# Second group's queries turned by TensorE products with the identity, and an earlier first rounding step of w_in: polysketch attention with an ELU feed-forward

## The chip, the cores and the metric

The kernel runs on one core of one Trainium2 chip. The metric is the device time of one execution in microseconds (us); the time before is the median of three runs. One further execution was recorded by the hardware profiler, and every view shown here comes from that one.

## The reference, cut to what matters

Sizes: batch 4, heads 4, sequence 1088, head dimension 32, sketch r = 8, d_model 128, d_ff 2048. q, k and v are float32; S1, S2, w_in and w_out come as float64.

```python
def phi(x):
    a = np.einsum('rd,bhsd->bhsr', S1, x)
    b = np.einsum('rd,bhsd->bhsr', S2, x)
    return np.einsum('bhsi,bhsj->bhsij', a, b).reshape(*x.shape[:-1], r * r)
q_p, k_p = (phi(q), phi(k))
kv = np.einsum('bhsf,bhsd->bhfd', k_p, v)
z = np.sum(k_p, axis=2)
num = np.einsum('bhsf,bhfd->bhsd', q_p, kv)
den = np.einsum('bhsf,bhf->bhs', q_p, z)[..., None] + 1e-06
attn_out = num / den
...
x = attn_out.transpose(0, 2, 1, 3).reshape(B * S, H * D)   # 4352 x 128
h = x @ w_in
g = np.where(h > 0.0, h, np.exp(np.minimum(h, 0.0)) - 1.0)
out = g @ w_out
```

## The kernel before, in words

The 4352 rows of x are handled in groups of 512 (a group is eight half tiles of 64 sequence positions with all four heads; the last group has 256). For a group the kernel works out the sketch of its queries, the denominator, the attention output x (tile `xg`, features on partitions), then in eight steps of two blocks of 128 hidden features each: `mm1` (h = w_in block times xg, tile `h`), the ELU on ScalarE (`elu_a`, tile `e`) and VectorE (`elu_d`, tile `gg`), and the second product into `o`, `pa` or `pb`. From the third group on, and for part of the second, the second product has seven block products in place of eight, with sums on POOL.

The order of the instructions is written out by hand: an engine runs its instructions in the order in which the Python code calls them, and waits for other engines by semaphores. Lines 952 to 1006 are the head, the loop at line 1107 is the steady part, in which tables (`at`, `mid`, `late`, lines 1015 to 1104) hang further work on a step's number.

The head, as far as it bears on the change:

- Loads go out on SP's queue in the order of lines 145 to 226: S, k, the first eight half tiles of q, v, the first w_in block (`load_w(0, 0)`), the other nine half tiles of q (line 215), the next w_in block, two w_out blocks, and so on. `hd_q` holds q with heads and 32 positions on partitions, `raw` the float64 words of a weight block.
- `transp` (line 281) turns q or k on VectorE, in blocks of 32x32, into `qT` or `kT` (head and feature on partitions).
- Weights are rounded from float64 to float32 in steps: `RA` (line 101, VectorE: the high word masked), `RB` (line 106, ScalarE), then on VectorE sign, mantissa, low word (lines 116, 120, 128: `RC_2` for the first two w_in blocks together) and the final product (line 136, `RE`).
- `KF`, `KO_*`, `Z*`: features of the keys of batch 0, their outer products (tile `kp`) and their sum. `KA` (line 428) has the 36 products of v with kp into tile `kv`, `KS_first` turns it (ScalarE copy `kd`, TensorE transpose, ScalarE copy `kvS`).
- First group: `q1_first` (tile `abq`), `q1z_first` (tile `zqp`), `q2_den` (line 603 `pw`, 608 and 609 `den`, 611 `an`: the division), `q2_out` (line 624, `qp`, two halves), `q4_early` (TensorE transposes `qtp`, ScalarE copies `qpT`, line 637), `q5_early` (products `xps`, ScalarE copies `xg`, line 649), `mm1_first` (tile `h`, line 257).
- Second group: `transp(qT, "q", 0, 8, NT)` turns half tiles 8 to 16 of batch 0, `q1_second` (line 537, tile `abwp`) uses half tiles 8 to 15.
- `keep_warm` gives TensorE products of ones into the tile `idle`, which nothing reads.

PSUM tiles with the tag `h` share four buffers, those with the tag `aux` two.

Of the kernel before, what the change touches and what calls it, by code (L numbers as in the profile page):

```python
# [12 lines left out]
F32 = mybir.dt.float32  # L13
# [9 lines left out]
def _ap(ap: bass.AP, free):  # L23
    return dataclasses.replace(ap, ap=[list(ap.ap[0])] + [list(x) for x in free])
# [3 lines left out]
def kernel(  # L28
# [21 lines left out]
    nc = tc.nc  # L50
    B, H, S, D = q.shape
    R = S1.shape[0]
    P = 128
# [4 lines left out]
    NT = S // 64  # L58
# [7 lines left out]
    psum = ctx.enter_context(tc.tile_pool(name="psum", bufs=2, space=bass.MemoryType.PSUM))  # L66


    hd = {}
# [3 lines left out]
    qT = [const.tile([FD, NT, 64], F32, name=f"qT{b}") for b in range(2)] * 2  # L73
# [104 lines left out]
    def round_w(f, i, *a):  # L178
        if wide:
            cp, w_in, w_out = order[i]  # L180
            c = slice(0 if w_in else 2 * P, 4 * P if w_out else 2 * P)
            f(raw_w[cp][:, c], W[:, cp, c], *a)

    def RA(i):
        round_w(round_a, i)

    def RB(i):
        round_w(round_b, i)


    def RC_2():
        if wide:
            for f in (round_s, round_m, round_d):
                f(raw_2[:, :, :2 * P], W[:, :2, :2 * P])
# [33 lines left out]
    ident = const.tile([P, P], F32, name="ident")  # L228
# [23 lines left out]
    width = [32]  # L252
# [8 lines left out]
    def keep_warm(n, cols=256, tile=P):  # L261
        ones = nc.const_aps.tensor(1.0, [P, 256], F32)
        for i in range(n):
            for c in range(0, P, tile):
                nc.tensor.matmul(idle[c:c + tile, :cols], ones[:, :tile], ones[:, :cols], skip_group_check=True,  # L265
                                 tile_position=(0, c))
# [13 lines left out]
    def transp(dst, x, b, t0, t1):  # L280
        nc.vector.transpose(dst[b][:, t0:t1, :].rearrange("p t (a c) -> p c t a", c=2), hd[x, b][:, :, t0:t1, :])


    SXh = const.tile([P, FD], F32, name="SXh")

    def make_SXh():
# [129 lines left out]
    def z_tile(b, ps, i):  # L416
        c = 32 * (i % 4)
        ab = feats[b]
        nc.tensor.matmul(ps[c:c + 32, R * R:R * R + H * R], ab[:, 0, i].rearrange("p h r -> p (h r)"),
                         ab[:, 1, i].rearrange("p h r -> p (h r)"), start=(b == 0 and i < 4), stop=(i >= KT - 4),  # L420
                         skip_group_check=True, tile_position=(0, c))

    def KA(b):
        kv = kv_ps[b] = psum.tile([P, 512], F32, name="kv", **(dict(tag="aux") if b else dict(tag="o1", bufs=1)))
        kp = [feats.pop((b, half)) for half in range(2)]
        for i in range(KT):
            for h in range(H):
                nc.tensor.matmul(kv[32 * h:32 * h + 32, :R * R], vt[b][:, (h * KT + i) * D:(h * KT + i + 1) * D],  # L428
                                 kp[i // 5][:, i % 5, h].rearrange("p i j -> p (i j)"),
                                 start=(i == 0), stop=(i == KT - 1), skip_group_check=True, tile_position=(0, 32 * h))  # L430
            if b:
                z_tile(b, kv, i)
# [42 lines left out]
            z_tile(0, ps, i)  # L475
        return ps, ZC(0, ps)

    def KS_first():
        kd = work.tile([P, 2, R * R], F32, name="kd", tag="kd", bufs=1)
        nc.scalar.copy(kd[:], _ap(kv_ps[0][:, :R * R], [[0, 2], [1, R * R]]))  # L480
        nc.tensor.transpose(kv_ps[0][:, 128:256], kd[:].rearrange("p w f -> p (w f)"), ident[:])
        nc.scalar.copy(kvS[:].rearrange("p h d -> p (h d)"), kv_ps[0][:, 128:256])

    def KV_first():
# [38 lines left out]
    def q1z_first():  # L523
        p = psum.tile([P, 512], F32, name="zqp", tag="h", bufs=4)
        for i in range(4):
            for u in range(2):
                b, t = half_tile(0, 2 * i + u)
                nc.tensor.matmul(p[64 * u:64 * u + 64, i * 32:i * 32 + 32].rearrange("p (h r) -> p h r", h=H),
                                 qT[b][:, t, :], SW[:, :, 2, :], skip_group_check=True, tile_position=(0, 64 * u))
        return p[:, :128].rearrange("p (t h r) -> p h t r", t=4, h=H)  # L530
# [65 lines left out]
    def q2_den(g, zq=None, between=None):  # L596
        m = H * (un[g] if g > 1 else qn[g])
        x = abw[g][:, :m, :]
        pw = pws[g % 2]
        if zq is None:  # L600
            nc.vector.tensor_mul(pw[:, :m, :R], x[:, :, R:2 * R], x[:, :, 2 * R:3 * R])
        else:
            nc.vector.tensor_mul(pw[:, :m, :R].rearrange("p (h t) r -> p h t r", h=H),
                                 x[:, :, R:2 * R].rearrange("p (h t) r -> p h t r", h=H), zq)
        if between:
            between()
        den = work.tile([P, 8 * H], F32, name="den", tag="den")
        nc.vector.tensor_reduce(den[:, :m], pw[:, :m], axis=AX, op=ADD)
        nc.vector.reciprocal(den[:, :m], den[:, :m])
        an = work.tile([P, 8 * H, R], F32, name="an", tag="an")  # L610
        nc.vector.tensor_mul(an[:, :m], x[:, :, R:2 * R], _ap(den[:, :m], [[1, m], [0, R]]))
        ans[g] = an

    def q2_out(g, parts=1, between=None):
        m = H * qn[g]
        x, an = abw.pop(g), ans.pop(g)
        qp[g] = work.tile([P, 4 * H, R, R], F32, name="qp", tag="qp", bufs=2)
        for i in range(parts):
            if i and between:
                between()  # L620
            h = slice(i * m // parts, (i + 1) * m // parts)
            a_ = an[:, h]
            b_ = x[:, h, :R]
            nc.vector.tensor_mul(qp[g][:, h], _ap(a_, list(a_.ap[1:]) + [[0, R]]),
                                 _ap(b_, [b_.ap[1], [0, R], b_.ap[2]]))

    def q4_early(g):

        qpT[g] = work.tile([P, H, 2, P], F32, name="qpT", tag="qpT", bufs=2)
        for hh in range(2):  # L630
            p = psum.tile([P, 512], F32, name="qtp", tag="aux")
            for h2 in range(2):
                for m in range(2):
                    o = (h2 * 2 + m) * P
                    r = (2 * hh + h2) * 4 + 2 * m
                    nc.tensor.transpose(p[:, o:o + P], qp[g][:, r:r + 2].rearrange("p t i j -> p (t i j)"), ident[:])  # L636
            nc.scalar.copy(qpT[g][:, 2 * hh:2 * hh + 2], p[:].rearrange("p (h m s) -> p h m s", h=2, m=2))

    def q5_early(g):
        xp = [psum.tile([P, 512], F32, name="xps", tag="aux") for _ in range(2)]  # L640
        for h in range(H):
            for w in range(2):
                nc.tensor.matmul(xp[w][D * h:D * h + D, :256], kvS[64 * w:64 * w + 64, h, :],
                                 qpT[g][64 * w:64 * w + 64, h].rearrange("p m s -> p (m s)"),
                                 skip_group_check=True, tile_position=(64 * w, D * h))
        xg[g] = work.tile([P, 512], F32, name="xg", tag="xg", bufs=3)
        to = xg[g][:].rearrange("p (m w s) -> p w m s", w=2, s=P)
        for w in range(2):
            nc.scalar.copy(to[:, w], xp[w][:, :256].rearrange("p (m s) -> p m s", s=P))  # L649
# [313 lines left out]
    KO_first(7, KT)  # L963
    keep_warm(1, 96, 64)
    zq = q1z_first()
    q2_den(0, zq, lambda: RA(0))
    q2_out(0, 2, lambda: RA(1))
    KA(0)
    KS_first()
    keep_warm(1)  # L970
    RB(0)
    RB(1)
    q4_early(0)
    transp(qT, "q", 0, 8, NT)
    RC_2()
    RE(0)
    RE(1)
    q1_second()
    q5_early(0)
    keep_warm(1, 192, width[0])  # L980
    mm1_first()
    q2(1, 2, lambda: RA(2))
    RB(2)
# [39 lines left out]
    def late(n, f, *a):  # L1023
        extra.setdefault((n, 1), []).append((f, *a))
# [28 lines left out]
    for b, (n_t, n_f, n_o, n_a, n_z) in enumerate(  # L1053
            ((4, 6, (7, 9), 11, 12), (15, 16, (17, 18), 19, 20), (19, 21, (23, 24), 27, 28)), 1):
        at(n_t, transp, kT, "k", b, 0, NT)
        at(n_f, KF_late, b)
        late(n_f, KF_late_out, b)
        for half in range(2):
            if b == 1:
                at(n_o[half], KO, b, half, nc.gpsimd)  # L1060
            else:
                late(n_o[half] - 1, KO_a, b, half)
                at(n_o[half], KO_b, b, half)
        at(n_a, KA, b)
        late(n_a, sums_out, b)
        at(n_z, turn, b)
        late(n_z, turned, b)
    late(10, transp, qT, "q", 1, 0, NT)
    at(21, transp, qT, "q", 2, 0, NT)
    late(24, transp, qT, "q", 3, 0, NT)  # L1070
# [36 lines left out]
    for n in range(2, N):  # L1107
        g, cp = steps[n]
# [29 lines left out]
        g, cp = before  # L1138
# [10 lines left out]
    g = NQ - 2  # L1149
# [53 lines left out]
```

## Time and profile before

| what | value |
|---|---|
| median of three runs | 265.38 us (265.32 to 265.83) |
| the profiled execution's own time | 265.08 us |
| its span, first to last instruction | 263.3 us |
| TensorE (PE) busy | 257.8 us, 98% |
| VectorE (DVE) busy | 188.2 us, 71% |
| ScalarE (ACT) busy | 184.5 us, 70% |
| GpSimd (POOL) busy | 168.2 us, 64% |
| mean granted TensorE clock | 1.000 |

The span is counted from the first instruction; all moments are us from there. In the busy tenths a row has 40 digits, one for each 6.6 us of the span, each the busy share of that slice in tenths. The chain of waits is the work that ended last, followed back from the last instruction: start, length, engine, tile and line. In the timeline a row has start, length, engine, line, operation, the tile written and those read, the shape and the count of instructions merged into it, and in brackets the idle time before it and what ended that. PE is a matmul, PEld the load of its stationary operand, SPq and ACTq are issues of DMAs. An f32 product counts as two instructions on PE.

### The profile page before, as it was taken

The numbers are of one execution on the slowest core, as the hardware profiler recorded it, in microseconds if no ns is written. First come the engines' busy times: TensorE is split into PE (matmuls) and PEld (weight loads), VectorE is DVE, ScalarE is ACT, GpSimd is POOL, SyncE is SP. The second block draws the span as 40 slices with busy tenths as digits, with TensorE's granted clock in tenths as the row PEclk, the third lists the DMA queues.
The fourth block names the chain that finished last, engine by engine and source line by source line (L and its number), as shares of the span: only waits on it lengthen the run. The fifth ranks groups of instructions, "written<-read, shape, count | busy, mean of one in ns | idle before, by whom it ended". The sixth has DMA issues, their size and how long they took to land.

```text
span 263.3 us, 9739 instructions
## 1 busy us (share of the span) xinstructions
PE 257.8 (98%) x4127; PEld 160.5 (61%) x4127; DVE 188.2 (71%) x349; ACT 184.5 (70%) x356; POOL 168.2 (64%) x251
## 2 busy tenths in 40 slices
PE   8899999999999999999999999999999999999994
PEld 7652334354346756667666666665666666667994
DVE  6899999997969997996477676644446445674651
ACT  2479978677567656775587777776777777777793
POOL 4400009105477996798869799888688888998300
PEclk9999999999999999999999999999999999999999
DMA  5997099020011110000100110011001100110011
GB/s 176 339 349 209 2 277 230 1 72 18 2 24 26 26 20 2 2 4 17 31 3 0 29 18 0 2 19 25 3 2 21 23 4 0 18 20 8 2 30 32
DMA packets 26442, 13.73 MB, mean 52 GB/s; under 512 B 19328, under 2 KB 24576, under 8 KB 26400
## 3 DMA queue, kind: packets, MB, share of 16 engines
q1 hardware_dynamic: 25968, 12.76, 18.9%
q8 instruction: 32, 0.52, 0.9%
q10 hardware_dynamic: 368, 0.30, 0.3%
q0 software_dynamic: 64, 0.07, 0.1%
q14 instruction: 10, 0.08, 0.1%
HBM read 10.88 MB, written 2.23 MB: 50 GB/s over the span
## 4 chain that ended last, share of the span: by engine, by line
PE 96%; POOL 1%; DVE 1%; ACT 1%; issue 0%
PE h L257 44%; PE pb L792 16%; PE pa L792 13%; PE o L257 5%; PE pb L768 4%; PE ol L257 3%; PE idle L265 1%; PE kv L428 1%; PE h L686 1%; PE qps L686 1%; POOL kp L324 1%; PE kfps L360 1%; PE qps L576 1%; PE qtp L636 1%; PE kv L257 1%; PE abp L341 1%
## 5 line engine op out<-in xcount | busy, mean ns | idle before, releaser
L257 PE MATMUL h<-xg,W 128*32 128x512 f32 (+3 forms) x904 | 130.7, 539 | 0.4 <-ACT xg L649 0.4
L875 DVE SCALAR_TENSOR_TENSOR gg<-e,h 128x512 f32<-128x512 f32 x128 | 85.6, 683 | 54.1 <-ACT e L869 50.6
L867 ACT ACTIVATE e<-h 128x512 f32<-128x512 f32 x128 | 75.5, 590 | 45.6 <-PE h L257 42.9
L869 ACT ACTIVATE e<-e 128x512 f32<-128x512 f32 x128 | 80.9, 632 | 3.8
L257 PEld LDWEIGHTS h<-xg,W 128*32 128x32 f32 (+1 forms) x904 | 42.6, 122 | 43.2 <-issue 34.9
L754 POOL TENSOR_TENSOR tt<-gg 128x256 f32<-128x256 f32 x50 | 37.0, 741 | 16.4 <-DVE gg L875 16.1
L751 POOL TENSOR_TENSOR tt<-gg 128x256 f32<-128x256 f32 x50 | 36.7, 734 | 5.5 <-DVE gg L875 5.1
L755 POOL TENSOR_TENSOR tt<-tt,gg 128x256 f32<-128x256 f32 x50 | 37.5, 750 | 3.9
L756 POOL TENSOR_TENSOR tt<-gg,tt 128x256 f32<-128x256 f32 x50 | 37.2, 744 | 3.9
L792 PEld LDWEIGHTS pa<-gg,W 128*64 128x64 f32 (+1 forms) x496 | 23.8, 125 | 23.5 <-issue 22.9
L792 PE MATMUL pa<-gg,W 128*64 128x128 f32 (+1 forms) x496 | 30.5, 274 | 0.0
L792 PE MATMUL pb<-tt,SS 128*64 128x128 f32 (+1 forms) x480 | 29.5, 273 | 0.0
L792 PEld LDWEIGHTS pb<-tt,SS 128*64 128x64 f32 (+1 forms) x480 | 22.6, 126 | 0.0
L792 PE MATMUL pa<-tt,SS 128*32 128x128 f32 (+1 forms) x288 | 21.0, 273 | 0.0
L133 POOL TENSOR_TENSOR raw<-raw,tiny 128x512 f32<-128x512 f32 x1 | 1.0, 1044 | 29.4 <-DVE raw L128 29.4
L792 PE MATMUL pb<-tt,W 128*64 128x128 f32 (+1 forms) x256 | 19.8, 273 | 0.0
L792 PE MATMUL pb<-gg,SS 128*64 128x128 f32 (+1 forms) x256 | 19.8, 273 | 0.0
L257 PE MATMUL o<-gg,W 128*32 128x512 f32 x128 | 15.3, 594 | 0.0
L792 PEld LDWEIGHTS pa<-tt,SS 128*32 128x32 f32 (+1 forms) x288 | 13.6, 124 | 0.0
L792 PEld LDWEIGHTS pb<-gg,SS 128*64 128x64 f32 (+1 forms) x256 | 12.7, 125 | 0.0
L792 PEld LDWEIGHTS pb<-tt,W 128*64 128x64 f32 (+1 forms) x256 | 12.6, 125 | 0.0
L768 PE MATMUL pb<-gg,W 128*32 128x256 f32 x192 | 11.5, 380 | 0.0
(163 smaller groups left out, 279.5 us busy)
## 6 DMA issues: line engine op xcount, KB each, us to landing
raw<-in_moe_w_in_dram SPq DMA_DIRECT2D x8, 256.0 KB, 6.6
raw<-in_moe_w_out_dram SPq DMA_DIRECT2D x8, 256.0 KB, 6.4
hd_k<-in_k_dram SPq DMA_DIRECT2D x3, 544.0 KB, 7.3
hd_q<-in_q_dram SPq DMA_DIRECT2D x3, 544.0 KB, 7.9
out_dram<-ob SPq DMA_DIRECT2D x88, 16.0 KB, 1.5
v<-in_v_dram SPq DMA_DIRECT2D x4, 288.0 KB, 6.8
v<-in_v_dram SPq DMA_DIRECT2D x4, 256.0 KB, 8.3
hd_k<-in_k_dram SPq DMA_DIRECT2D x1, 288.0 KB, 3.3
```

Source lines behind the costliest of these rows:

```text
L257: nc.tensor.matmul(dst[c:c + tile], lhs[:, c:c + tile], rhs, skip_group_check=True, tile_position=(0, c), **kw)
L265: nc.tensor.matmul(idle[c:c + tile, :cols], ones[:, :tile], ones[:, :cols], skip_group_check=True, tile_position=(0, c))
L686: nc.tensor.matmul(ps[w][s * r:s * r + s, 64 * k:64 * (k + m)], lhs, qpT[g, i][rows, o + 2 * k:o + 2 * (k + m), f, :], start=(f == 0 and j ...
L751: nc.gpsimd.tensor_tensor(t[:, 0], b12, b11, op=SUB)
L754: nc.gpsimd.tensor_tensor(t[:, 2], b22, b12, op=SUB)
L755: nc.gpsimd.tensor_tensor(t[:, 1], t[:, 2], b11, op=ADD)
L756: nc.gpsimd.tensor_tensor(t[:, 3], b21, t[:, 1], op=SUB)
L768: nc.tensor.matmul(acc[1][0][r:r + width[0], 256 * hi:256 * hi + 256], lhs[:, w:w + width[0]], gg[:, c, 256 * u:256 * u + 256], start=(cp ...
L792: nc.tensor.matmul(bank[r:r + width[0], P * col:P * col + P], lhs[:, w:w + width[0]], rhs[:, u], start=(first and i in ((0,) if g == 1 els ...
L867: nc.scalar.activation(e, hs[g, cp][c][:, :n], RELU, scale=-1.0)
L869: nc.scalar.activation(e, e, EXP, scale=-1.0)
L875: nc.vector.scalar_tensor_tensor(gs[g, cp][:, c, :n], es[g, cp][:, c, :n], -1.0, hs[g, cp][c][:, :n], op0=ADD, op1=MAX)
```

## The change

Half tiles 8 to 15 of the first batch's queries are no longer turned by VectorE in the head. `turn_q` turns them on TensorE: for each half tile, each half of it and each head one 32x32 product of the q block with the identity, 32 in each of two calls, all into one PSUM tile `qtu` of 128x512; `turn_q_out` copies each half of that tile (128x256) on ScalarE into `qT`. Half tile 16, which the second group doesn't use, is turned by VectorE in step 3 of the loop. One `keep_warm` is left out and another has 128 columns in place of 192. `RA(0)` is called ahead of `q2_den`, where it stood between the division's first product and its sum. `RB(0)` is called ahead of `KA`, and the copy to `kvS` (`KS_first_b`) stands between the two ScalarE copies `qpT` of the first group.

```diff
--- before.py
+++ after.py
@@ -281,6 +281,23 @@
         nc.vector.transpose(dst[b][:, t0:t1, :].rearrange("p t (a c) -> p c t a", c=2), hd[x, b][:, :, t0:t1, :])
 
 
+
+    def turn_q(t0, t1):
+        if not turned_q:
+            turned_q.append(psum.tile([P, 512], F32, name="qtu", tag="h", bufs=4))
+        for t in range(t0, t1):
+            for c in range(2):
+                for h in range(H):
+                    r = slice(D * h, D * h + D)
+                    o = 64 * (t - 8) + 32 * c
+                    nc.tensor.matmul(turned_q[0][r, o:o + 32], hd["q", 0][r, c, t, :], ident[r, r],
+                                     skip_group_check=True, tile_position=(D * h, D * h))
+
+    def turn_q_out(t0, t1, copy=nc.scalar.copy):
+        copy(qT[0][:, t0:t1, :].rearrange("p t (a c) -> p t a c", c=2),
+             turned_q[0][:, 64 * (t0 - 8):64 * (t1 - 8)].rearrange("p (t c a) -> p t a c", c=2, a=32))
+
+    turned_q = []
     SXh = const.tile([P, FD], F32, name="SXh")
 
     def make_SXh():
@@ -475,10 +492,12 @@
             z_tile(0, ps, i)
         return ps, ZC(0, ps)
 
-    def KS_first():
+    def KS_first_a():
         kd = work.tile([P, 2, R * R], F32, name="kd", tag="kd", bufs=1)
         nc.scalar.copy(kd[:], _ap(kv_ps[0][:, :R * R], [[0, 2], [1, R * R]]))
         nc.tensor.transpose(kv_ps[0][:, 128:256], kd[:].rearrange("p w f -> p (w f)"), ident[:])
+
+    def KS_first_b():
         nc.scalar.copy(kvS[:].rearrange("p h d -> p (h d)"), kv_ps[0][:, 128:256])
 
     def KV_first():
@@ -624,7 +643,7 @@
             nc.vector.tensor_mul(qp[g][:, h], _ap(a_, list(a_.ap[1:]) + [[0, R]]),
                                  _ap(b_, [b_.ap[1], [0, R], b_.ap[2]]))
 
-    def q4_early(g):
+    def q4_early(g, between=None):
 
         qpT[g] = work.tile([P, H, 2, P], F32, name="qpT", tag="qpT", bufs=2)
         for hh in range(2):
@@ -635,6 +654,8 @@
                     r = (2 * hh + h2) * 4 + 2 * m
                     nc.tensor.transpose(p[:, o:o + P], qp[g][:, r:r + 2].rearrange("p t i j -> p (t i j)"), ident[:])
             nc.scalar.copy(qpT[g][:, 2 * hh:2 * hh + 2], p[:].rearrange("p (h m s) -> p h m s", h=2, m=2))
+            if between and hh == 0:
+                between()
 
     def q5_early(g):
         xp = [psum.tile([P, 512], F32, name="xps", tag="aux") for _ in range(2)]
@@ -963,21 +984,24 @@
     KO_first(7, KT)
     keep_warm(1, 96, 64)
     zq = q1z_first()
-    q2_den(0, zq, lambda: RA(0))
+    RA(0)
+    q2_den(0, zq)
     q2_out(0, 2, lambda: RA(1))
+    RB(0)
     KA(0)
-    KS_first()
-    keep_warm(1)
-    RB(0)
+    turn_q(8, 12)
+    KS_first_a()
+    turn_q_out(8, 12)
+    turn_q(12, 16)
+    turn_q_out(12, 16)
     RB(1)
-    q4_early(0)
-    transp(qT, "q", 0, 8, NT)
+    q4_early(0, KS_first_b)
     RC_2()
     RE(0)
     RE(1)
     q1_second()
     q5_early(0)
-    keep_warm(1, 192, width[0])
+    keep_warm(1, 128, width[0])
     mm1_first()
     q2(1, 2, lambda: RA(2))
     RB(2)
@@ -1065,6 +1089,7 @@
         late(n_a, sums_out, b)
         at(n_z, turn, b)
         late(n_z, turned, b)
+    late(3, transp, qT, "q", 0, 16, NT)
     late(10, transp, qT, "q", 1, 0, NT)
     at(21, transp, qT, "q", 2, 0, NT)
     late(24, transp, qT, "q", 3, 0, NT)
```

## The prediction

> **What bounds the kernel now.** I read four views in this order. First the page's busy tenths, which say in which stage which engine is full:
>
> ```profile
> PE   8899999999999999999999999999999999999994
> ...
> PEclk9999999999999999999999999999999999999999
> ```
>
> TensorE is full from the third slice (13 us) on, at a granted clock of 1.0. Every part of the change except one small transpose lies in the first two and a half slices, so the question is what sets the moment from which TensorE runs without a pause. The chain of waits gives that moment:
>
> ```profile
> 12.52 0.14 issue
> 12.65 0.63 PE qtp L636 x4
> 13.28 0.85 PE abwp L537 x16
> 14.13 0.70 PE xps L643 x16
> 14.83 0.64 ACT xg L649 x2
> 15.47 0.11 issue
> 15.58 2.79 PE h L257 x40
> ```
>
> From h at 15.58 us the chain stays on TensorE to the last step; read instruction by instruction, TensorE has no idle stretch above 0.03 us after 15.58 until 60 us and later. So what moves 15.58 moves the end by as much. Just ahead of it the chain is ScalarE's copy xg, ahead of that the products xps, then abwp, which reads qT of the second group. The timeline shows how close the rival input is:
>
> ```profile
> 9.43 1.21 PE L428 MATMUL kv<-kp,v 128*32 128x64 f32 x72
> 9.62 0.29 DVE L603 TENSOR_TENSOR pw<-abq,zqp 128x128 f32<-128x128 f32 x1 [0.23 <-PE zqp L528]
> 9.82 0.33 DVE L101 TENSOR_SCALAR W<-raw 128x256 uint32<-128x256 uint32 x1
> ...
> 10.07 0.29 DVE L608 TENSOR_REDUCE den<-pw 128x16 f32<-128x144 f32 x1
> ...
> 12.42 0.77 DVE L281 STREAM_TRANSPOSE qT<-hd_q 128x576 f32<-128x576 f32 x1
> ...
> 13.31 0.59 ACT L637 COPY qpT<-qtp 128x512 f32<-128x512 f32 x1 [0.28 <-PE qtp L636]
> ...
> 14.81 0.65 ACT L649 COPY xg<-xps 128x256 f32<-128x256 f32 x2 [0.15 <-PE xps L643]
> 15.01 0.76 DVE L136 SCALAR_TENSOR_TENSOR W<-raw,W 128x256 f32<-128x256 f32 x2
> ```
>
> VectorE's first weight block is done at 15.43 (half of the 0.76 us row), xg at 15.46: h waits for two engines that arrive within 0.03 us of each other. Relieving one alone brings nothing. The reader should also see that L101, the step RA(0) that the change moves, lies between pw and den and that VectorE was idle for 0.23 us before pw. Last, the landing of what RA(0) reads (its load is issued at 3.90 us):
>
> ```profile
> DMA to landing us min/median/max: 5.7/5.7/5.7
> ```
>
> It lands at 9.60, so the idle 0.23 us (9.39 to 9.62) is not free for RA(0).
>
> **What the Trainium skill says.** "TensorE: Matmul & The Clock Gate", Part 3, says that small matmuls at different tile positions overlap, with some 4 ns from tile to tile. The trace agrees for column tiles (four kv products start 7 ns apart, and the next four 55 ns later); it has no 32x32 tiles. "TensorEngine Tiling (Array Packing)", Gotcha 1, says that different row tiles cannot access one PSUM bank at the same time. The four heads of turn_q are four row groups writing one bank, though other partitions of it; no run here shows that. "VectorE: DVE Perf Modes", The DRAIN you can't avoid: the next operation starts when the pipe is empty, earlier when it isn't held. Here pw to L101 is 0.20 us, but a dependent step 0.32 (den to reciprocal). "ScalarE: Activation LUTs", What ACT_TABLE_LOAD costs: back-to-back ACTIVATEs overlap by about 93 ns; in the trace 0.10 (two xg copies of 0.37 start 0.27 apart).
>
> **The change part by part.**
>
> *RA(0) ahead of pw.* It can start at 9.60 plus the 0.07 us from landing to start (first k tile: 4.5 to 4.57), about 9.69. pw follows 0.25 later (as den follows L101 now), at 9.94, and den 0.32 after pw, at 10.26 instead of 10.07. So the move costs VectorE 0.19 us: between pw and den RA(0) lay half in a wait that had to be waited anyway. Behind the waiting RA(0) stand pw, the division and both qp halves; the second qp ends at 12.69 instead of 12.50. If the load lands 0.2 us earlier the move costs nothing, if 0.2 later 0.4.
>
> *The VectorE transpose taken out* (0.77 us at 12.42). RC_2 can follow qp at 12.69, but waits for RB(1) on ScalarE, below. VectorE is ahead of TensorE there in the end, so this gain of up to 0.5 us goes to waiting.
>
> *turn_q, twice 32 products.* An f32 product is two instructions (36 kv products stand as x72), so twice 64. In sets of four tiles that is 16 sets. The nearest row is zps, also 32 columns and 32-wide: eight instructions in two sets, the sets 0.033 us apart. kv, with 64 columns, has 0.055. I take 0.033, keep 0.055 as the upper bound, and as the lower 0.025, the floor that the TensorE page gives for a start-to-start (Wait — 56ns, not 53.3ns?). A turn is then 15 x 0.033 = 0.50 to the last start, plus 0.20 for that instruction (zps row): 0.70. The first start is 10.57: last kv start 10.42 plus the 0.15 that zqp to kv shows for another tile shape. hd_q must be there: its load is the next after RA(0)'s, 288 KB, and the loads around it land 0.7 us per 256 KB apart, so about 10.4 (estimate). That fits by 0.15 us; later landings are paid one for one, with kd's transpose and all of qtp queued behind.
>
> *The new waits.* The built program shows the second turn_q waiting for a ScalarE semaphore, and the only new ScalarE step between is the first turn_q_out: both use one bank. So the halves do not overlap. The chain, with a release of 0.07 us to ScalarE (kv end 10.64 to kd 10.71) and 0.05 to TensorE (kd end 10.98 to 11.03), and 0.37 us for a copy (abq and xg halves, also 128x256):
> - first turn 10.57 to 11.27; copy 11.34 to 11.71;
> - second turn 11.76 to 12.46; copy from 12.53;
> - on ScalarE in order, each start a duration less 0.10 later: RB(1) 12.80 (0.51), qpT 13.21 (0.59), kvS 13.70 (0.27), second qpT 13.87, done 14.46, instead of 13.90.
>
> TensorE keeps up: qtp can start at 12.4 and its second half at 12.9 (qp is there at 12.69, so RA(0)'s 0.19 is hidden), abwp runs 13.5 to 14.4. Then xps at 14.51, xg 0.75 later as now (14.06 to 14.81), h 0.77 after xg as now: 16.03. RC_2 after RB(1) starts at 13.34 instead of 13.12, weights at 15.65, ahead of xg (15.91). **h moves from 15.58 to 16.03, +0.45 us.** kvS is moved behind the first qpT and RB(0) ahead of kd; RB(0) needs 10.05 to 10.56, just before kd at 10.71, and costs nothing, the 0.17 of kvS is in the list. The removed keep_warm (0.60 us) and the narrower second one fill pauses and set no end.
>
> *The rest transpose in step 3* (128x64): the transposes shown fall by 0.9 ns per element, so 0.25 us, 0.2 after overlap. VectorE has no pause from 28.74 to 62.65 us, so all of that is late by 0.2 against TensorE. The smallest margins I find: weights finished by POOL at 42.08 for h at 42.49, and the h buffer freed at 49.37 for h at 49.80. 0.4 covers 0.2: zero, at most 0.1. On SP, the q load of batch 2 now waits for this transpose (about 29.6) and is issued at 34.73 after loads that wait until 32.06 anyway: zero.
>
> Sum: profiled execution 265.08 (span 263.3 and 1.8 around) + 0.45 = 265.53. The median is 0.30 above the profiled one, so 265.38 + 0.45 = **265.83**, +0.17%. A measurement of this kernel tells about 0.2% (0.53 us) from no change; the forecast lies just inside.
>
> **The rivals.**
> - *VectorE was the bound after all* and the rest hides: RC_2 at 12.54 instead of 13.12, h 0.58 earlier: 264.8, faster. For it: the two inputs are 0.03 apart. Against: the release is xg's, and xg gets longer. 0.05.
> - *A cheaper turn:* sets of 0.025 us, an early landing, copies overlapping better: h between -0.4 and +0.2, about 265.4. 0.15.
> - *The turn is slower than zps*: one mechanism, the pace of the 32x32 products in a shared bank. Each ns per set costs 2 x 15 ns, so from 0.036 us per set on the kernel is over 0.2% slower; at kv's 0.055 it is +1.11, 266.5 (0.17); if the row groups take turns on the bank, 64 x 0.033 = 2.1 us per turn instead of 0.5, +3.2, 269.0 (0.09). For it: the bank rule above, and no such tile in the trace. Against: distinct partitions.
> - *The clock falls*, since 0.6 us of full-array products give way to 32x32 ones (the same page, Part 1: activity in windows of about 3.4 us): one such window at half speed, +1.7, 267.5. 0.04. The idle stretches would stay below 0.5 us, about as now.
>
> **How the numbers follow.** The forecast case has 0.50, about 265.5 to 266.1; landing times and copies mostly err upward, so 0.20 of it counts as slower and 0.30 as same. Same: 0.30 + 0.15 = 0.45. Slower: 0.20 + 0.17 + 0.09 + 0.04 = 0.50. Faster: 0.05. The range 265.2 to 266.7 leaves out the first rival, the shared bank and the clock: 0.18.
>
> **What would show it.** Right: RA(0) at about 9.7 with pw behind it near 9.9; qtu in two bursts of 0.7 us with 0.45 between; the second qpT copy ending at 14.4 to 14.5; h at 16.0; no pause of TensorE at 42 and 50 us. Wrong: h at or before 15.6, bursts over 0.8 us, a clock under 1.0, or h right but the end moved by another amount.

## The result, and the profile after

The changed kernel takes 271.63 us (median of six runs, 271.16 to 274.67), the kernel before 265.48 us (six runs beside it): ratio 1.0249, 95% interval 1.0204 to 1.0294. The forecast was 265.83 us with a range of 265.2 to 266.7. The profiled execution of the changed kernel took 271.71 us, its span is 269.9 us, its mean granted clock 0.987.

The page of the changed kernel, busy tenths and one DMA queue. Before, the first row begins with 8899 and the second has nothing but 9s:

```profile
PE   8679999999999999999999999999999999999994
PEclk9959999999999999999999999999999999999999
...
q8 instruction: 33, 0.54, 0.8%
```

TensorE now has holes in the second and third slices (6.7 to 20.2 us), and its clock reads 5 in the third. Everything from the fourth slice on looks as before. The third line is a queue that the prediction never read: 33 packets in 0.54 MB, so 16 KB each, of the kind "instruction" (before: 32).

The chain of waits of the changed kernel, from the first turn to the first products h (start, length, what):

```profile
11.35 3.47 issue
14.82 0.56 PE qtu L293 x21
...
15.83 1.08 PE qtu L293 x64
16.91 1.90 PE qtp L655 x8
18.80 1.48 PE abwp L556 x16
20.28 0.85 PE xps L664 x16
...
21.36 0.56 issue
...
22.34 2.58 PE h L257 x39
```

The chain reaches h at 22.34 us where before it did at 15.58: +6.76, against +0.45 forecast. The largest piece is the first row, 3.47 us of "issue": TensorE stands still *in the middle of the first turn*, with products on both sides that have the same kind of inputs, and no other engine is named. A stop that ends on nothing in the profile and falls inside a run of like instructions points away from a wait for data.

Its place becomes plain by counting. This is the view of busy time by stretch, with the number of instructions that started in each (x), first for the changed kernel and then for the kernel before:

```profile
0.00:12.00 12.00, 9.90 (x221) 8.08 (x221) 8.77 (x32) 3.88 (x9) 6.16 (x27) 1.00 0.81 242
0.00:21.50 21.50, 16.37 (x348) 12.75 (x348) 12.76 (x41) 7.11 (x17) 6.16 (x27) 0.84 0.93 279
```

```profile
0.00:14.60 14.60, 12.87 (x221) 9.89 (x221) 11.49 (x37) 6.03 (x14) 6.09 (x27) 1.00 0.86 269
```

The stop comes after 221 products and 221 weight loads (with a few semaphore records, 449 records of TensorE). The shorter stop at 21.36 comes after 348 and 348, 254 later (256 with the other records). The kernel before reaches the same count of 221 and 221 exactly at the end of xps, its next product starts at 14.65, and only a keep_warm stands behind it: a stop there would have been hidden, since h waits for xg until 15.58 (experiment 6 shows that there was none).

**Theory F** that follows: TensorE's instructions reach it in blocks of 256 over the DMA queue of 16-KB packets, and it stops where the next block has not come. The trace times the packets. This is the queue in the changed kernel from 12.0 to 13.5 us: one packet, and 4.7% of 16 engines' 1.5 us is 1.13 us.

```profile
q8 instruction: 1, 0.02, 4.7%
```

Read packet by packet, it takes 12.21 to 13.34 us, and TensorE goes on at 14.82; the next takes 19.03 to 20.49 and TensorE goes on at 21.92. In both, TensorE resumes some 1.45 us after the packet's end. In the kernel before the packet took 11.96 to 13.09 us, so it came at much the same time. That the queue is TensorE's is seen from its count, which goes with TensorE's instructions: 32 packets with 4159 products and as many weight loads (experiment 7), 33 with 4189 (experiment 4), while the counts of VectorE, ScalarE and GpSimd differ by two at most. The two turns issue 128 instructions and as many weight loads, 256 records more ahead of h: what used to lie ahead of the boundary now lies behind it. "Runtime: NRT & Kernel Launch", Instruction fetch mechanics, in the Trainium skill describes such blocks of 256 instructions fetched ahead by the sequencer, and calls the cost of a boundary "mostly hidden". The block size agrees with the count here; "mostly hidden" holds for the later boundaries, since the timeline shows no pause of TensorE from 22.4 to 70 us, but not for the one at 14.82, after a stop of 3.47 us.

The rival theories before the experiments: the turn is dear by itself (32x32 tiles, the shared bank, the copies); or the moved steps cost; or it is the clock alone.

### The profile page after: what moved, and what is told of

It reads as the page before. It is cut to its first block, busy times and chain, and to the rows that moved or that the text cites. A ratio compares the mean times of both kernels' runs of the same rounds, so it can differ in the third digit from the quotient of the medians.

```text
span 269.9 us, 9996 instructions
## 1 busy us (share of the span) xinstructions
PE 260.9 (97%) x4253; PEld 163.7 (61%) x4253; DVE 187.9 (70%) x349; ACT 185.2 (69%) x358; POOL 168.2 (62%) x251
## 3 DMA queue, kind: packets, MB, share of 16 engines
HBM read 10.88 MB, written 2.23 MB: 49 GB/s over the span
## 4 chain that ended last, share of the span: by engine, by line
PE 95%; issue 2%; DMA 1%; ACT 0%; DVE 0%; SPq 0%; DVEq 0%
PE h L257 43%; PE pb L813 16%; PE pa L813 13%; PE o L257 5%; PE pb L789 4%; PE ol L257 3%; PE kv L445 2%; DMA hd_k<-in_k_dram 1%; PE h L707 1%; PE qtp L655 1%; PE qps L707 1%; PE qtu L293 1%; PE abp L358 1%; PE kfps L377 1%; PE qps L595 1%
```

## The experiments

All ratios are to the kernel before on the same chip, with 95% intervals.

**1. The kernel before with as many idle products.** No turn, nothing moved:

```diff
     KA(0)
+    keep_warm(16, 32, 32)
     KS_first()
```

> The kernel before with 64 products of ones (128 rows, 32-wide, 32 columns) into the unused tile after the 36 kv products: as many TensorE instructions more (256) as turn_q has, but no turn, no read of hd_q, no 32x32 tiles, no new wait. Theory F (TensorE waits for its own next block of instructions, whose load sits behind the kernel's loads): TensorE stops at the same count of recorded instructions as in the changed kernel, 449, here after about 43 of the 128 product instructions, at 11.0 to 11.3 us, and goes on at about 14.6, as soon as the block is there; the clock falls to half from about 14; total 270.5 to 272. Theory T (the turn itself stops: 32x32 tiles in one bank, or hd_q not landed): no stop, the products fill pauses, total 265.4 to 266.2.

Measured 271.0 us (270.29 to 271.58), ratio 1.0204 (1.018 to 1.0227). By stretch, and then in the chain of waits:

```profile
0.00:12.00 12.00, 10.06 (x221) 8.26 (x222) 8.85 (x33) 3.37 (x8) 6.07 (x27) 1.00 0.81 242
```

```profile
10.75 0.40 PE idle L265 x38
11.16 3.58 issue
14.74 1.27 PE idle L265 x85
```

Products that read only a constant stop at the same count for 3.58 us and go on at 14.74. The clock fell as well (means of 0.992 to 0.994 in all four runs). So neither q, nor the turn's tiles, its bank or its copies are needed for the loss; 128 more TensorE instructions there, with their weight loads, are enough.

**2. The changed kernel with the later loads held back.** If the packet is late because the DMA engines are full (their share in the stretch from 10.58 to 14 us reads 1.08; packets are counted where they start, so it can pass 1, and all 16 are at work), fewer loads should bring it sooner. SP issues the loads from the second block's w_out on, so both w_out blocks and all that follows, only after the first group's qp:

```diff
-    load_w(1, 1)
-    load_w(0, 1)
-    for b in range(1, B):
+    def later_loads():
+        nc.vector.memset(raw_2[:, 1, 2 * P:2 * P + 1, :].rearrange("p c w -> p (c w)").bitcast(F32), 0.0)
+        load_w(1, 1)
+        load_w(0, 1)
+        for b in range(1, B):
...
     q2_out(0, 2, lambda: RA(1))
+    later_loads()
```

> The changed kernel with the loads from the second block's w_out on issued only after the first group's qp (a write of two words by VectorE holds SP's queue until about 12.7 us), so that the DMA engines run empty from about 11 us. Theory F: the block of instructions is no longer behind other loads, the stop of 3.47 us falls to under 1.7 us and the clock stays at 1.0; total 266 to 268. Theory T: the stop stays at 3 to 3.6 us with the half clock behind it; total 271 to 272, more if the weights come late.

Measured 271.09 us, ratio 1.02 (1.0172 to 1.0228). The timeline of TensorE (in brackets the idle time and what ended it):

```profile
12.48 0.38 PE L295 MATMUL qtu<-ident,hd_q 32*32 32x32 f32 x21 [0.77 <-issue]
...
19.92 0.42 PE L259 MATMUL h<-xg,W 128*32 128x256 f32 x4 [2.81 <-DVE W L136]
```

The stop stood at the same count and shrank from 3.47 to 0.77 us (the packet took 10.04 to 11.15 us): that half was as expected. The time and the clock were not (0.5 from 20.50 to 23.92 us, in the profiled execution, where 1.0 was expected): the w_out words go to the same tile as the w_in words, and VectorE's L116 waited 4.40 us for their loads. The edit bought one wait with another, so its time says nothing; experiment 5 mends it.

**3. The moved steps alone.** RA(0) ahead of `q2_den`, RB(0) ahead of `KA`, the kvS copy between the qpT copies; no turn, VectorE's transpose and both keep_warms as before:

```diff
-    q2_den(0, zq, lambda: RA(0))
+    RA(0)
+    q2_den(0, zq)
     q2_out(0, 2, lambda: RA(1))
+    RB(0)
     KA(0)
-    KS_first()
+    KS_first_a()
     keep_warm(1)
-    RB(0)
     RB(1)
-    q4_early(0)
+    q4_early(0, KS_first_b)
```

> The change without the turn: RA(0) ahead of pw, RB(0) ahead of kv, kvS between the two qpT copies; the second group's queries are turned by VectorE as before and both keep_warm are as before. Theory F: 449 instructions are reached as before, no stop in the way; the moves cost 0 to 0.3 us (RA(0) waits for its load, pw and the division 0.2 later): 265.4 to 265.8. Rival (the reordering carries a good part of the loss): over 266.5.

Measured 265.57 us, ratio 1.0002 (0.9993 to 1.0012), clock 1.0 to within 0.002. The moves are free to within 0.3 us. In the profiled execution the head ran 0.5 us late from zqp on (9.36 against 8.84), and record 449, there the last of the xps products, came at 15.07, 0.25 us behind its neighbour: a short stop, which was not expected and which the time doesn't show.

**4. The changed kernel with 32 products fewer ahead of the turn.** Only 4 of the 36 products of v with kp of the first batch are made, so the attention of batch 0 leaves most keys out. That takes away 64 instructions and 64 weight loads:

```diff
-        for i in range(KT):
+        for i in range(KT if b else 1):
```

> The changed kernel with 4 of the 36 kv products of the first batch (only the first of nine key tiles is summed; the others are left out), so 128 TensorE instructions fewer ahead of the turn. Theory F: TensorE again stops after 449 recorded instructions, which is now 42 products' worth of instructions into the second turn, at about 12 us, for 2.3 to 3 us. Theory T: it stops where it did, after 43 of the first turn's 64 product instructions, for about 3.5 us.

Measured 269.61 us (one run):

```profile
12.02 0.57 PE L293 MATMUL qtu<-ident,hd_q 32*32 32x32 f32 x42 [0.21 <-ACT qT L297]
14.58 0.54 PE L293 MATMUL qtu<-ident,hd_q 32*32 32x32 f32 x22 [1.99 <-issue]
```

The stop went with the count, from the first turn into the second, and ended at 14.58, nearly the same moment as before. It is not tied to any one instruction. With a single run, the time itself says little.

**5. Experiment 2 mended.** The first two blocks' w_out words have a tile of their own, so that VectorE doesn't wait for them:

```diff
+        raw_o = const.tile([P, 2, 2 * P, 2], U32, name="rawo")
...
-            f(raw_w[cp][:, c], W[:, cp, c], *a)
+            f(raw_o[:, cp] if cp < 2 and not w_in else raw_w[cp][:, c], W[:, cp, c], *a)
...
+    later_loads()
```

> As e2_after_light, but the first two blocks' w_out words land in a tile of their own, so that the rounding of w_in no longer waits for them (that wait, 4.4 us, is what took the place of the shortened stop there). Theory F: TensorE stops after 449 recorded instructions for about 1 us as in e2, the clock stays at 1.0 and h starts 1.4 to 1.6 us later than in the kernel before with the same loads (0.45 forecast for the turn, about 1 for the stop): 266.4 to 267.3. If the stop were of the turn itself: 271 to 272.

Measured 267.07 us (266.95 to 267.94), ratio 1.0059 (1.0043 to 1.0076). TensorE's timeline:

```profile
12.28 0.38 PE L297 MATMUL qtu<-ident,hd_q 32*32 32x32 f32 x21 [1.05 <-issue]
```

The packet took 9.77 to 10.89 us and TensorE went on 1.39 after it. The same program around the turn, with only the loads moved, has lost 4.6 of its 6.2 us. The clock was not as expected: in the profiled run (267.94) it was 0.5 from 14.40 to 17.81. The other three runs, at clocks of 0.998 to 1.0, took 266.95, 266.95 and 267.19.

**6. The control: the kernel before with those loads and that tile.**

```diff
+        raw_o = const.tile([P, 2, 2 * P, 2], U32, name="rawo")
...
     q2_out(0, 2, lambda: RA(1))
+    later_loads()
     KA(0)
```

> The control of e5: the kernel before with the same later loads and the same tile for w_out. Both theories: no change, 265.2 to 265.9; its TensorE reaches 449 recorded instructions at about 14.3 us, when the block has long been there, so the 0.3 us pause after it goes.

Measured 265.48 us, ratio 1.0004 (0.9988 to 1.002). Holding the loads back is neither a gain nor a loss by itself; it helps only a kernel that stops. One part of the expectation failed: there was no pause to go. In the profiled execution the products after record 449 begin 0.59 us after the first xps (14.83 and 15.42), although the block had come at 11.22; in the kernel before it is 0.59 too (14.06 and 14.65). So the kernel before didn't stop there.

**7. and 8. The kernel before with fewer idle products**, `keep_warm(4, 32, 32)` and `keep_warm(1, 32, 32)` at the place of experiment 1, so that the count runs out ahead of abwp, or within xps:

```diff
     KA(0)
+    keep_warm(4, 32, 32)
     KS_first()
```

> The kernel before with 16 products of ones after the 36 kv products (64 TensorE instructions instead of the 256 of e1). Theory F: record 449 is now the last one ahead of abwp, reached at 13.2 us; abwp waits until about 14.6, h comes 1.2 to 1.5 us later, the pause is too short for the clock: 266.5 to 267.1. Theory T: 265.4 to 265.7.

> The kernel before with 4 products of ones after the 36 kv products (16 TensorE instructions). Theory F: record 449 falls into the xps products, the second half of which then starts at about 14.6 instead of 14.3: 265.6 to 265.9. Theory T: 265.4 to 265.5.

With 16 products 266.54 us (266.27 to 267.14), ratio 1.0044 (1.0028 to 1.006); with 4 products 265.51, ratio 1.0003 (0.9992 to 1.0014). TensorE in the first of the two, then in the second:

```profile
14.75 0.88 PE L537 MATMUL abwp<-SW,qT 128*64 128x96 f32 x16 [1.33 <-DVE raw L120]
...
16.74 0.64 PE L257 MATMUL h<-xg,W 128*32 128x256 f32 x8
```

```profile
14.18 1.03 PE L643 MATMUL xps<-qpT,kvS 64*32 64x256 f32 x16
```

The first is the case to remember: the bracket names VectorE's L120, and abwp, which reads SW and qT, doesn't need it. The trace names what it can; the count (221 and 221 again) and the moment 14.75 tell that the block was late. h came 1.16 later (16.74 against 15.58; zqp, far ahead of the stop, was 0.14 late already), the time was 1.05 longer, at a clock of 1.0: this is the price of a stop alone. In the second, xps is stretched from 0.66 to 1.03; h came at 15.69, 0.11 later, and zqp was 0.13 late, so the stop reached h by nothing that can be seen. The time is 0.02 longer, with an interval from -0.2 to +0.4 us, which doesn't exclude the 0.1 to 0.4 expected.

**9. Experiment 5 with idle products in its pauses**, to keep the clock up:

```diff
     turn_q(8, 12)
+    keep_warm(1, 64)
     KS_first_a()
+    keep_warm(1, 192)
     turn_q_out(8, 12)
     turn_q(12, 16)
+    keep_warm(1, 192)
     turn_q_out(12, 16)
```

> This is the changed kernel with light loads (the one whose stop was 1.05 us and whose clock fell to 0.5 for 3.41 us, 267.07 us) with three products of ones over the full array put into its pauses: 64 columns after the first turn, 192 after the transpose of kd, 192 after the second turn. Nothing of the computation is left out. Theory F with the clock as a second cost: the stop after 449 recorded TensorE instructions stays at about 1.0 us; the products raise TensorE's full-array time between 11 and 14.4 us by about 1 us, so the clock stays at 1.0 and h starts 0.8 to 1.2 us earlier than its 18.31, at 17.1 to 17.5: 266.0 to 266.4. Rival, the clock follows the stop itself and not how much of the array is busy: 0.5 for a window again, 267.0 or more.

Measured 267.41 us (267.07 to 267.79), ratio 1.0069 (1.0052 to 1.0086). The clock was 1.0 (0.998 to 1.0), as the first theory said, and the time was not shorter, which it had not said. Two reasons, both visible: three of the four runs of experiment 5 already had the full clock, so there was little to win, and the run doesn't decide between the two theories of the clock; and the idle products stood in the way. The second turn could have started 0.05 after the copy's end at 13.57:

```profile
13.20 0.37 ACT L301 COPY qT<-qtu 128x256 f32<-128x256 f32 x1 [1.65 <-PE qtu L297]
...
13.89 0.75 PE L297 MATMUL qtu<-ident,hd_q 32*32 32x32 f32 x64
```

It started at 13.89, behind the 192 columns of ones that began at 13.46 and took 0.49, and h came at 18.09 in place of the 17.1 to 17.5 expected. I had priced the clock from one profiled run.

**10. and 11. As many idle products as in experiment 1, in the steady part**, at first in step 6, into a tile with the tag `aux`:

```diff
         mm1(g, cp)
         for f, *a in extra.get(n, ()):
             f(*a)
+        if n == 6:
+            pad = psum.tile([P, 512], F32, name="pad", tag="aux")
+            ones = nc.const_aps.tensor(1.0, [P, 256], F32)
+            for c in list(range(0, P, 32)) * 16:
+                nc.tensor.matmul(pad[c:c + 32, :32], ones[:, :32], ones[:, :32], skip_group_check=True,
+                                 tile_position=(0, c))
```

> The kernel before with 64 added products of ones, 128x32 to 32 columns in four column tiles (128 instructions, as many as in the two turns), put into step 6 of the steady part, where few loads are under way. Theory F: the added instructions only matter where the next block is not there yet; in the steady part TensorE takes about 10 us for 256 recorded instructions, so there is no stop and only their own pace is paid, 32 sets of 0.033 us, 1.1 us: 266.4 to 266.8. Rival, so many small products cost the same wherever they are (a cost of their own, 5.5 us as after KA in the first experiment): 270 or more.

Measured 271.84 us, ratio 1.023 (1.0198 to 1.0262): the rival's number, and for another reason than the rival's.

```profile
41.12 1.28 PE L1116 MATMUL pad<-const-float32-1.0 128*32 128x32 f32 x127 [3.79 <-DVE abk L370]
```

The products waited for a buffer: step 6 has just put the key features into both `aux` buffers, and VectorE turns them only at 40.6 us. This bracket is a true one, since the first of abk's two transposes ended just ahead of the products and the count is at no boundary. Behind the wait the clock was 0.5 from 42.29 to 45.71. The experiment measured a buffer and tells nothing of F. So it was made again in step 3 (`n == 3`), where both buffers are free:

> The kernel before with 64 added products of ones, 128x32 to 32 columns in four column tiles (128 TensorE instructions and as many weight loads, as many as in the two turns and in the first experiment), at 26.1 us, ahead of the second block's products into o, where no other engine holds the tile that they write. Theory F: the block of instructions that they run into has come by then (packets at 24.5 to 25.9 us, few other loads), so there is at most a short stop, and only their own pace is paid, 32 sets of 0.033 us, 1.1 us: 266.4 to 266.9, clock 1.0. Rival, so many small products cost the same wherever they are, by themselves and through the clock: 270 or more, as after KA.

Measured 266.71 us (266.47 to 266.87), ratio 1.0047 (1.003 to 1.0064), clock 0.999 to 1.0.

```profile
26.08 1.29 PE L1116 MATMUL pad<-const-float32-1.0 128*32 128x32 f32 x126
27.77 0.19 PE L1116 MATMUL pad<-const-float32-1.0 128*32 128x32 f32 x1 [0.40 <-issue]
```

The same products that cost 5.5 us after `KA` cost 1.35 here, about their own 1.1 us (an estimate, 32 sets of 0.033) and a stop of 0.40. Even that stop fits F: it comes after record 961, which is 449 + 2 x 256, and ends 1.27 after the packet that took 25.41 to 26.50.

**12. Half of the turn, at the count of before.** Half tiles 12 to 15 are turned on TensorE, 8 to 11 on VectorE after the first group's queries, and only 4 of the 36 products of v with kp are made (the attention of batch 0 leaves most keys out, as in experiment 4), which takes away what the turn adds:

```diff
     KA(0)
-    turn_q(8, 12)
     KS_first_a()
-    turn_q_out(8, 12)
     turn_q(12, 16)
     turn_q_out(12, 16)
     RB(1)
     q4_early(0, KS_first_b)
+    transp(qT, "q", 0, 8, 12)
```

> The changed kernel with the turn of only four of the eight half tiles on TensorE (12 to 15; 8 to 11 by VectorE after the first group's queries, as before), and with only 4 of the 36 products of v with kp of the first batch (the other 32 left out, so that the attention of batch 0 leaves most keys out). The turn adds 64 instructions and 64 weight loads and the left-out products take as many away, so the count of TensorE instructions ahead of h is that of before. Theory F: no stop within the turn or ahead of xps, h between 15.2 and 16.0, clock 1.0: 265.0 to 265.8. Rival, the 32x32 turn itself, or its copy, is what costs: half of the change's loss stays, 267.5 to 269.

Measured 265.41 us (264.74 to 267.02, 20 runs), ratio 1.0009 (0.9997 to 1.0022).

```profile
10.79 0.75 PE L293 MATMUL qtu<-ident,hd_q 32*32 32x32 f32 x64
...
14.17 0.66 PE L664 MATMUL xps<-qpT,kvS 64*32 64x256 f32 x16
```

A turn of 64 instructions runs in 0.75 us in one piece, TensorE has no stop that ends in "issue", h is at 15.39. So the turn itself, in this half of it, is not what costs. These 20 runs also price the clock: 12 with a mean clock of 0.997 or more took 264.74 to 265.49 (mean 265.17), 8 with 0.993 or 0.994 took 265.95 to 267.02 (mean 266.40), 1.23 us more. A mean of 0.9935 is what one window of 3.41 us at half clock gives in 263 us (an estimate); where it lay in those 8 runs is not on record, and the expected clock of 1.0 came in the other 12 only.

## Why the prediction was wrong

**The step that failed** is "turn_q, twice 32 products ... so twice 64": the count was right and only its execution was priced. 128 instructions and their weight loads also have to be delivered. The prediction took for granted that an instruction is there when its inputs are. Five kernels with full loads show the price: whatever stands behind record 449 starts no sooner than 14.6 to 14.8 us (14.82 in the changed kernel, 14.74, 14.58 and 14.75 in experiments 1, 4 and 7; in experiment 8 it falls inside xps, at 14.57). In the kernel before only a keep_warm stood behind it, and TensorE came to it at 14.65, when the block was there. The change put the rest of the first turn, kd's transpose, the second turn, qtp, abwp and xps behind it.

**The sum by its own terms**, in the profiled execution:
- first turn from 10.78 where 10.57 was forecast: +0.21. zqp started at 9.05 where before it was 8.84, at 8.81 to 9.57 in the other kernels. It differs from execution to execution; here the turning of k had begun 0.16 later (4.73 against 4.57);
- its end at 15.35 (14.82 + 0.53) where 11.27 was forecast, a length of 4.57 in place of 0.70: +3.87, the stop;
- from there to h 6.99 (22.34 less 15.35) in place of 4.76: +2.23. TensorE's rows say why. Second turn, qtp, abwp and xps took 1.08, 1.97, 1.55 and 0.92 us; at full clock they took 0.75, 1.09, 0.88 and 0.66 (the turn and xps in experiment 12, qtp and abwp in experiment 2). That is 2.14 more, and these rows follow each other without a pause:

```profile
15.83 1.08 PE L293 MATMUL qtu<-ident,hd_q 32*32 32x32 f32 x64
16.84 1.97 PE L655 MATMUL qtp<-ident,qp 128*128 128x128 f32 x8
18.73 1.55 PE L556 MATMUL abwp<-SW,qT 128*64 128x96 f32 x16
20.21 0.92 PE L664 MATMUL xps<-qpT,kvS 64*32 64x256 f32 x16
```

Together 6.31; the time was 6.18 over the forecast for a profiled execution (271.71 less 265.53). The second stop, 0.56, lies within the last term and adds at most 0.3 there: xg was done at 21.90 and h followed 0.44 later, where before it followed after 0.12.

**The clock** was a rival at 0.04, "one such window at half speed, +1.7", with "the idle stretches would stay below 0.5 us". In the changed kernel it happened behind the stop:

```profile
10.58:14.00 3.42, 0.77 (x63) 0.57 (x51) 2.08 (x6) 0.27 (x1) 0.00 (x0) 1.00 1.08 365
14.00:20.82 6.82, 5.93 (x126) 4.57 (x126) 2.58 (x5) 2.97 (x7) 0.00 (x0) 0.50 1.08 325
```

In the 3.42 us ahead of the drop TensorE was busy for 0.77 us, and the clock (second last but one column) was 0.50 for twice 3.41 us. "TensorE: Matmul & The Clock Gate", Part 1, gives the window as 3413 ns, and the transitions in this trace lie multiples of 3.41 us apart. Its price was high in the forecast: 1.23 by experiment 12, 0.9 by the runs of experiment 5 (267.94 against a mean of 267.03). "Removed keep_warm ... set no end" is right for time on the path. Experiment 1 keeps these products and loses clock all the same, so a long stop is enough. It isn't the only way, though. In experiment 4 the clock fell at 12.61, when the stop had only just begun (12.59), and 8 of the 20 runs of experiment 12 had the low clock in a kernel whose profiled execution shows no stop; in experiment 3, which keeps the idle products and all of kv, none of 13 had it. Experiments 4 and 12 leave out a keep_warm and 32 kv products, so the forecast's reason, that TensorE has less full-array work, may have a share; which of the two matters isn't shown.

**What held.** RA(0) ran at 9.66 and pw at 9.93 where 9.69 and 9.94 were forecast; the copies took 0.37; the second turn waited for the first copy; the 32x32 sets started 0.032 to 0.033 us apart, so the rival of a slow or shared bank is false: four row groups wrote into one bank, in other partitions, as fast as zps (0.033), with starts 7 ns apart in products of 0.24 us. "TensorEngine Tiling (Array Packing)", Gotcha 1, on row tiles and a bank, isn't borne out for this case. The moves cost nothing that could be measured (experiment 3). The transpose in step 3 took 0.24 us, and TensorE has no pause from 22.4 to 70 us. With a short stop and the full clock, experiment 5 lies 1.5 us above before (266.95 to 267.19 against 265.48), which is about the forecast's 0.45 and the stop's 1.05. So +0.45 for the rest of the change agrees, though no run shows it alone at full size.

**What stays open.** When TensorE asks for a block isn't in the trace, only when the packet runs. What the clock counts as activity isn't settled: in experiment 7 a window with TensorE busy for 1.84 us did not lower it; in experiments 5 and 4 windows with 2.14 and 2.31 us, mostly of 32x32 tiles and transposes, did. And two runs of the changed kernel with one window at half clock by the mean (0.993 and 0.994) took 271.53 and 271.56, within the 271.16 to 274.67 of those with two; where that window lay wasn't recorded. So 2.23 is in the main what half speed cost in the profiled execution, not in every one.

## What to carry to other kernels

Ahead of a change that adds many small TensorE instructions, count products and weight loads up to the place and look for boundaries every 256 records, with the packets of the instruction queue beside them: what stands behind a boundary starts no sooner than its block, however soon its inputs come. Where the first boundary lies is to be read from the kernel's own trace: here it is record 449, 63 short of twice 256, and what the other 63 are isn't in the trace. A long "issue" inside a run of like instructions, or a bracket that names an engine whose result isn't needed, is to be checked against that count. While the loads fill the DMA engines a block is late, and small instructions use up blocks fastest: 128 instructions of 1.1 us in all cost 5.5 us in the head, half clock included, and 1.35 us in the steady part.

## What the runs showed of the hardware that was not expected

- TensorE stopped after the same 449 records in eight kernels (the changed one and experiments 1, 2, 4, 5, 7, 8 and 9), with 221 products and 221 or 222 weight loads among them, whatever the instructions were; in the changed kernel again 256 later, and in experiment 11 512 later.
- It went on 1.3 to 1.5 us after the end of the 16-KB packet, which itself took 1.1 to 1.5 us. With the DMA engines full the packet of the first boundary ran within 12.0 to 13.5 us, with the later loads held back within 9.7 to 11.4.
- A clock of 0.5 came in whole windows of 3.41 us, once with a stop of only 1.05 us, once just as one began (experiment 4), and a window of it cost 0.9 to 1.2 us in experiments 5 and 12.
